# Forming P-Q on VectorE and GpSimd instead of in a third TensorE pass

## The chip, the cores and the metric

The kernel runs on one core of a Trainium2 chip. The metric is the device time of one execution in microseconds (us). The core's engines are TensorE (PE in the profile, with its weight loads as PEld), VectorE (DVE), ScalarE (ACT), GpSimd (POOL) and SyncE (SP). Each engine works through its own queue of instructions in the order of the program, and semaphores tie the queues together.

## The reference

```python
def _attn_ref(x):                       # x: (8, 3008, 256)
    X = np.fft.fft(x, axis=1)
    X = np.fft.fft(X, axis=2)
    return X.real

def _moe_ref(x, w_in, w_out):           # x: (24064, 256), w_in: (256, 2048), w_out: (2048, 256)
    h = np.maximum(x @ w_in, 0.0)
    return h * h @ w_out
```

The output of the first is reshaped to 24064 tokens of 256 and given to the second. So the real part of a two-dimensional Fourier transform of each of 8 batches goes through a feed-forward layer with a squared Relu.

## The kernel before

The real part of the transform splits into a part made of cosines, Zc, and a part made of sines, Zs. Row k of the result has P + Q as its product with `w_in`, and the mirrored row S - k has P - Q, where P comes from Zc and Q from Zs. The transform along the 256 dimensions is folded into the weights once: `gh[:, 0]` holds the cosine table times `w_in`, `gh[:, 1]` the sine table times `w_in`, each 128 x 2048, and `gh[:, 2]` is `gh[:, 1]` times -2. One row is different: partition 0 of Zs and of `gh[:, 1]` is used for the cosine part of d = 128, whose product has the same sign in both rows of a pair; there `gh[:, 2]` is 0 (`turn2`).

Columns. Only half of the 3008 rows of a batch are computed as columns (1505 a batch, 12040 in all); each column gives two rows of the output. The columns are cut into 25 windows: six of 240, 512, 376, 376, 512 and 448 columns (`FIRST`), then 18 full ones of 512 (windows 6 to 23, counted from 0) and a last one of 360.

A window. The hidden layer's 2048 features are 16 chunks of 128, handled in pairs by 8 pair steps, s = 0 to 7:

- `pq(s)`: for each of the two chunks a matmul of `gh[:, 0]` with Zc (`zcw`, L684) and one of `gh[:, 1]` with Zs (`zsw`, L685) into a PSUM tile `ph` of two banks: P + Q. There are two such tiles.
- `square(s, 0)`: ScalarE takes Relu of `ph` into `h1` (L694, three buffers), VectorE squares it into the first half of `h2` (L696).
- `others(s)`: work that is interleaved: steps of the fold of a later batch (`at[s]`), one eighth of the second matmul of the window before (`ffn2_steps`, L596; ScalarE copies two groups of its result at a time to `osb`, L611, and SyncE stores it), then `post[s]`, then matmuls that make Zc and Zs of the next window (`z_steps`, L478, L483, L487; VectorE's part is `minus`, L494).
- `turn(s)`: two matmuls of `gh[:, 2]` with Zs onto the same `ph` (L690), which makes it P - Q.
- `square(s, 1)`: Relu and square again, with the columns reversed, into the second half of `h2`.

The order is written out by hand (`manual_schedule`): each engine gets its instructions in the order of the program text.

The fold. Before its transform each batch is folded by symmetries into smaller inputs. In windows 5, 8, 10, 13, 16 and 19 (`fold_at`) a batch is folded beside the pair steps: step 0 has `d_even` (VectorE: `fe`, L349), step 1 `n_cos` (`ab`, L358), step 2 `d_odd` (`fo`, L353), step 3 `n_sin` (`ab`, L361), step 4 `odds` (`od`, L368). `d_odd` also issues the load of the next batch's `x` on GpSimd's queue (`load_x`, L125, L130, and L141 or L147 for batches at an edge), into a single buffer that `fo` is the last to read. `post[5]` has `nyq`: two small matmuls of TensorE on `od` (L373, L374). Step 6 has `even` (VectorE: `ev`, L379; GpSimd's queue stores it to DRAM as `scr`, L381), step 7 `back` (GpSimd's queue reads it back as `rb`, L389, L391). In windows 6, 9, 12, 15, 18 and 21 (`late_at`) steps 2 to 5 have the second stage of the fold (`fold8`, `fold16`, L404, L415, and small copies on GpSimd, L421 to L423).

Of the kernel before, what the change touches and what calls it, by code (L numbers as in the profile page):

```python
# [8 lines left out]
F32 = mybir.dt.float32  # L9
F16 = mybir.dt.float16  # L10
I32 = mybir.dt.int32
AF = mybir.ActivationFunctionType
ALU = mybir.AluOpType

HS = 32.0
P = 128
# [3 lines left out]
def rev_dim(ap, i):  # L20

    dims = [list(d) for d in ap.ap]
    step, cnt = dims[i]
    dims[i] = [-step, cnt]
    return bass.AP(tensor=ap.tensor, offset=ap.offset + step * (cnt - 1), ap=dims)
# [3 lines left out]
def kernel(  # L29
# [14 lines left out]
    nc = tc.nc  # L44
    B, S, D = x.shape
    _, F = moe_w_in.shape
# [7 lines left out]
    NFC = F // P  # L54
    WN = 512

    FIRST = [240, 512, 376, 376, 512, 448]
    R23 = float(2.0 ** 23)

    RQ = (1, 3, 5, 0, 2, 4)  # L60

# [11 lines left out]
    wins = []  # L73
# [5 lines left out]
    NW = len(wins)  # L79

    def win_of(col):
        return max(w for w in range(NW) if wins[w][0] <= col) if col < TOT else NW
# [17 lines left out]
    const = ctx.enter_context(tc.tile_pool(name="const", bufs=1))  # L100
    tmp = ctx.enter_context(tc.tile_pool(name="tmp", bufs=2))
# [7 lines left out]
    drp = ctx.enter_context(tc.tile_pool(name="drp", bufs=2, space=bass.MemoryType.DRAM))  # L109
    ps_h = ctx.enter_context(tc.tile_pool(name="ps_h", bufs=2, space=bass.MemoryType.PSUM))  # L110
    ps_o = ctx.enter_context(tc.tile_pool(name="ps_o", bufs=2, space=bass.MemoryType.PSUM))
# [56 lines left out]
    perm = [const.tile([P, P], F16, name=f"perm{i}") for i in range(2)]  # L168
# [3 lines left out]
    nc.gpsimd.memset(idx["c"][0:2, :], P - 3)  # L172
    idx["f"] = iota([P, 1], [[1, 1]], -1, 1, "idx_f")
    nc.gpsimd.memset(idx["f"][0:1, :], 0)
    w16 = [const.tile([P, 2, F // 2], F16, name=f"w16_{i}") for i in range(2)]
    for i in range(2):
        nc.gpsimd.dma_start(out=w16[i], in_=moe_w_in[:, i * F // 2 : (i + 1) * F // 2].rearrange("(c p) f -> p c f", p=P))
    wout16 = const.tile([P, NFC, D], F16, name="wout16")
# [2 lines left out]
    def small(shape, name):  # L181
        return const.tile(shape, F32, name=name)
# [22 lines left out]
    def table_steps(e):  # L205
# [19 lines left out]
        def args(h):  # L225
            t = st["t", h] = tmp.tile([P, 3, NE], F32, name="t", tag="tt")
            for j in range(nr):
                r = row(h, j)
                if e == 0:
                    nc.scalar.activation(t[:, j, 0:n], st["kf"], AF.Copy, bias=R23, scale=vs[:, r : r + 1])  # L230
                else:
                    nc.vector.tensor_scalar(out=t[:, j, 0:n], in0=st["kf"], scalar1=vs[:, r : r + 1], scalar2=R23, op0=ALU.mult, op1=ALU.add)

        def turns(h):
            t = st["t", h]
            nc.vector.tensor_scalar(out=t[:, 0:nr, 0:n], in0=t[:, 0:nr, 0:n], scalar1=-R23, scalar2=-float(S), op0=ALU.add, op1=ALU.mult)

# [44 lines left out]
    at = const.tile([P, 2, P + 1], F32, name="at")  # L282
    for c in range(2):
        nc.scalar.activation(at[:, c, :], drow, AF.Copy, bias=R23, scale=dvs[:, c : c + 1])
    nc.vector.tensor_scalar(out=at, in0=at, scalar1=-R23, scalar2=-float(D), op0=ALU.add, op1=ALU.mult)
    for c in range(2):
# [141 lines left out]
    gh = const.tile([P, 3, F], F16, name="gh")  # L428
# [17 lines left out]
    def gh_turn(cc):  # L446
        f0 = cc * 512
        nc.vector.tensor_scalar(out=gh[:, 2, f0 : f0 + 512], in0=gh[:, 1, f0 : f0 + 512], scalar1=turn2[:, 0:1], scalar2=None, op0=ALU.mult)
# [3 lines left out]
    def zwin(w):  # L452
        if w not in zc:
            zc[w] = zp.tile([P, WN], F16, name="zc", tag="zc")
            zs[w] = zp.tile([P, WN], F16, name="zs", tag="zs")
        return zc[w], zs[w]
# [101 lines left out]
    for cc in range(1, F // 512):  # L558
        gh_turn(cc)

    def store(osb, p0, g0, m, minus, eng=nc.sync):

        for b, k0, kstep, n, c0 in runs:
            il, ih = max(g0, c0) - c0, min(g0 + m, c0 + n) - 1 - c0
            if minus and k0 in (0, H):
                il = max(il, 1)
            cnt = ih - il + 1
            if cnt <= 0:
                continue
            if minus:  # L570
                lo = p0 + (m - 1) - (c0 + ih - g0)
                row = b * S + S - (k0 + kstep * ih)
            else:
                lo = p0 + c0 + il - g0
                row = b * S + k0 + kstep * il
            eng.dma_start(
                out=bass.AP(tensor=out.tensor, offset=out.offset + row * D, ap=[[kstep * D, cnt], [1, D]]),
                in_=osb[lo : lo + cnt, :])
# [51 lines left out]
    def fold_jobs(i):  # L630
        f = folds[i] = fold_steps(i)
        return [f["d_even"], f["n_cos"], f["d_odd"], f["n_sin"], f["odds"], f["nyq"], f["even"], f["back"]]

    fold_at, late_at = {}, {}
    for i in range(2, B):
        fold_at[win_of(col_of[i, 0]) - 2] = i
        late_at[win_of(col_of[i, 1]) - 2] = i
    NST = NFC // 2
    old = None
    for w in range(NW):  # L640
        g0, wn = wins[w]
        h2 = h2p.tile([P, NFC, 2 * WN], F16, name="h2", tag="h2")
        zcw, zsw = zwin(w)

        lo, hi = 0, NST - 1
        at = [[] for _ in range(NST)]
        post = [[] for _ in range(NST)]
        if w == 0:
            at[2] = [f0s["even"], f0s["back"]]
        elif w == 1:  # L650
            fj = fold_jobs(1)
            at = [[f] for f in fj[0:5]] + [[], [], []]
            post[5] = fj[5:6]
            lo, hi = 6, 7
        elif w == 2:
            te = table_steps(1)
            at = [[folds[1]["even"], lambda: te["freq"](), lambda: te["args"](0)], [lambda: te["turns"](0)], [lambda: te["mods"](0)],
                  [lambda: te["absm"](0)], [lambda: te["sins"](0)], [lambda: te["coss"](0)], [], [lambda: te["weigh"]()]]
            for st in range(4):
                at[st + 3] = at[st + 3] + f0s["late"][st : st + 1]  # L660
            at[7].append(folds[1]["back"])
        elif w in fold_at:
            fj = fold_jobs(fold_at[w])
            at = [[f] for f in fj[0:5]] + [[], fj[6:7], fj[7:8]]
            post[5] = fj[5:6]
        elif w == win_of(col_of[1, 1]) - 1:
            for st in range(4):
                at[st] = folds[1]["late"][st : st + 1]
            lo = 4
        if w in late_at:  # L670
            for st in range(4):
                at[st + 2] = at[st + 2] + folds[late_at[w]]["late"][st : st + 1]
        zj, zl = [], []
        for u in need[w + 1]:
            zu = z_steps(u)
            zj += [(zu, 0, 0), (zu, 1, 0), (zu, 0, 1), (zu, 1, 1)]
        f2 = ffn2_steps(*old) if old else []
        phs = {}

        def pq(s):  # L680
            ph = phs[s] = ps_h.tile([P, 2, 512], F32, name="ph", tag="psh")
            for a in range(2):
                f0 = (2 * s + a) * P
                nc.tensor.matmul(ph[:, a, 0:wn], gh[:, 0, f0 : f0 + P], zcw[:, 0:wn], start=True, stop=False)  # L684
                nc.tensor.matmul(ph[:, a, 0:wn], gh[:, 1, f0 : f0 + P], zsw[:, 0:wn], start=False, stop=True)  # L685

        def turn(s):
            for a in range(2):
                f0 = (2 * s + a) * P
                nc.tensor.matmul(phs[s][:, a, 0:wn], gh[:, 2, f0 : f0 + P], zsw[:, 0:wn], start=False, stop=True, skip_group_check=True)  # L690

        def square(s, sg):
            h1 = h1p.tile([P, 2, 512], F16, name="h1", tag="h1")
            nc.scalar.activation(h1[:, :, 0:wn], phs[s][:, :, 0:wn], AF.Relu)  # L694
            hv = rev_dim(h1[:, :, 0:wn], 2) if sg else h1[:, :, 0:wn]
            nc.vector.tensor_tensor(h2[:, 2 * s : 2 * s + 2, sg * wn : (sg + 1) * wn], hv, hv, op=ALU.mult)  # L696

        def others(s):
            for j in at[s]:
                j()  # L700
            for j in spread(f2, s, NST):
                j()
            for j in post[s]:
                j()
            if s == lo:
                zl[:] = [j for zu, part, h in zj for j in zu(part, h)]
            if s >= lo:
                for j in spread(zl, s - lo, hi - lo) if s < hi else []:
                    j()


        ng = 2 if w == 0 or wins[w - 1][1] < 384 < wn else 1
        for s0 in range(0, NST, ng):
            ss = range(s0, s0 + ng)
            for s in ss:
                pq(s)
            for s in ss:
                square(s, 0)
            others(s0)
            for s in ss:  # L720
                turn(s)
            for s in ss:
                square(s, 1)
            for s in ss[1:]:
                others(s)
        old = (w, h2)
    for j in ffn2_steps(*old, tail=True):
        j()
# [30 lines left out]
```

## Time and profile before

| | before |
|---|---|
| median of 3 runs | 633.65 us (633.65, 633.65, 635.58) |
| profiled execution, span from first to last instruction | 632.0 us |
| TensorE, matmuls | busy 615.9 us (97%) |
| ScalarE | busy 457.4 us (72%) |
| VectorE | busy 369.5 us (58%) |
| GpSimd | busy 76.5 us (12%), nearly all of it issuing DMAs |
| granted TensorE clock | 1.000 |

The time of the profiled execution itself is known as its span; the median of the runs is 1.65 us above it. A line of the profile's groups gives the source line, the engine, the operation, output and inputs by name, their shapes and the count, then the busy time, the mean duration of one instruction in ns, and the idle time of its engine before it with what ended that. A line of the timeline gives the start in us from the start of the span, the duration in us, the engine, the line, the operation and how many of them are merged, and in brackets the idle time before and its releaser. Matmuls are pipelined: one of 128x512 is shown with 379 ns, but the next starts 0.21 us after it.

### The profile page before, as it was taken

The page shows a single profiled execution, that of the slowest core. Times are in us where ns is not written, and L with a number is a line of the kernel's source. Part 1 is how long each engine was busy: PE and PEld are TensorE (multiplying, and loading weights), DVE is VectorE, ACT ScalarE, POOL GpSimd, SP SyncE. Part 2 cuts the span into 40 slices and gives each one's busy share as a digit, 9 for nine tenths or more (in the row PEclk, how much of TensorE's full clock was granted, in tenths as well). Part 3 has the DMA queues.
Part 4 walks back from the last instruction along what each step waited for, and adds up shares of the span by engine and source line. Part 5 has one row for each costly group of instructions (what it writes and reads, how often), then busy time and mean ns, then how long its engine had stood idle before and what let it go on. Part 6 is the DMA issues. An engine that isn't in the chain of part 4 may idle for free.

```text
span 632.0 us, 11586 instructions
## 1 busy us (share of the span) xinstructions
PE 615.9 (97%) x4548; PEld 439.1 (69%) x4548; DVE 369.5 (58%) x604; ACT 457.4 (72%) x610; POOL 76.5 (12%) x125
## 2 busy tenths in 40 slices
PE   5899999999999999999999999999999999999997
PEld 2457776776777767767777677777677776777786
DVE  7887656765457557645576455854557555454430
ACT  7787778777777677767777777777777777777662
POOL 5352200022002200220011100030000200000000
PEclk9999999999999999999999999999999999999999
DMA  8936211172112711631127211262111311111112
GB/s 146 211 82 127 85 34 34 50 164 78 36 43 58 184 46 42 144 97 35 51 44 160 74 52 39 59 151 73 40 31 55 111 34 47 38 46 35 49 54 65
DMA packets 36525, 47.52 MB, mean 75 GB/s; under 512 B 4216, under 2 KB 30328, under 8 KB 36472
## 3 DMA queue, kind: packets, MB, share of 16 engines
q0 software_dynamic: 9344, 22.14, 17.6%
q1 hardware_dynamic: 26899, 24.44, 12.7%
q8 instruction: 35, 0.57, 0.4%
q10 hardware_dynamic: 228, 0.21, 0.1%
q14 instruction: 19, 0.15, 0.1%
HBM read 33.63 MB, written 27.84 MB: 97 GB/s over the span
## 4 chain that ended last, share of the span: by engine, by line
PE 93%; DVE 3%; ACT 2%; issue 1%; POOL 0%; ACTq 0%; POOLq 0%; DVEq 0%
PE po L596 51%; PE ph L684 12%; PE ph L685 12%; PE ph L690 12%; PE pz L478 4%; ACT h L694 1%; PE pw L301 1%; DVE h L696 1%; PE pg L436 0%; ACT cos L259 0%; DVE fe L349 0%; DVE fo L353 0%; ACT sin L248 0%; ACT gh L440 0%; DVE od L368 0%
## 5 line engine op out<-in xcount | busy, mean ns | idle before, releaser
L694 ACT ACTIVATE h<-ph 128x1024 f16<-128x1024 f32 (+4 forms) x400 | 368.4, 974 | 80.0 <-PE ph L690 72.1
L696 DVE TENSOR_TENSOR h<-h 128x1024 f16<-128x1024 f16 (+4 forms) x400 | 262.4, 660 | 231.6 <-ACT h L694 228.2
L596 PE MATMUL po<-wout,h 128*128 128x256 f16 (+1 forms) x3024 | 361.6, 273 | 0.0
L596 PEld LDWEIGHTS <-h 128*128 128x128 f16 (+1 forms) x3024 | 296.8, 98 | 71.3
L684 PE MATMUL ph<-zc,gh 128*128 128x512 f16 (+4 forms) x400 | 145.9, 366 | 1.1 <-ACT h L694 0.8
L685 PE MATMUL ph<-zs,gh 128*128 128x512 f16 (+4 forms) x400 | 145.9, 366 | 0.4 <-ACT zs L487 0.4
L690 PE MATMUL ph<-zs,gh 128*128 128x512 f16 (+4 forms) x400 | 112.8, 366 | 2.0 <-ACT h L694 1.5
L611 ACT ACTIVATE osb<-po 128x512 f32<-128x512 f32 (+3 forms) x95 | 54.9, 582 | 57.4 <-PE po L596 52.4
L685 PEld LDWEIGHTS <-gh 128*128 128x128 f16 x400 | 39.1, 98 | 43.8 <-issue 2.5
L684 PEld LDWEIGHTS <-gh 128*128 128x128 f16 x400 | 39.0, 98 | 41.8 <-issue 0.5
L690 PEld LDWEIGHTS <-gh 128*128 128x128 f16 x400 | 37.2, 97 | 12.7 <-issue 4.3
L421 POOL COPY xt<-xt 128x2 f16<-128x2 f16 x16 | 2.5, 186 | 173.2 <-DVE xt L404 173.2
L130 POOL DMA_INDIRECT xo<-in_x_dram,idx_r x15 | 22.1, 1471 | 4.6 <-issue 4.6
L125 POOL DMA_DIRECT2D xo<-in_x_dram x8 | 6.0, 751 | 109.8 <-DVE fo L353 109.8
L483 ACT ACTIVATE es<-pz 128x376 f32<-128x376 f32 (+1 forms) x32 | 15.4, 481 | 5.3 <-PE pz L478 5.2
L391 POOL DMA_INDIRECT rb<-scr,idx_r x16 | 18.5, 1158 | 4.9 <-issue 4.9
L487 ACT ACTIVATE zs<-pz 128x376 f16<-128x376 f32 (+23 forms) x27 | 8.5, 358 | 9.9 <-PE pz L478 9.9
L349 DVE TENSOR_TENSOR fe<-xo 128x3072 f16<-128x3072 f16 x8 | 14.3, 1786 | 1.6 <-DMA xo<-in_x_dram,idx_r 1.3
L353 DVE TENSOR_TENSOR fo<-xo 128x3072 f16<-128x3072 f16 x8 | 14.2, 1779 | 0.0
L494 DVE SCALAR_TENSOR_TENSOR zc<-es,pz 128x376 f16<-128x376 f32 (+20 forms) x26 | 9.4, 392 | 7.2 <-ACT zc L487 7.0
L301 PE MATMUL pw<-spn 128*128 128x384 f16 x30 | 8.2, 448 | 5.2 <-DVE spn L290 5.2
L389 POOL DMA_DIRECT2D rb<-scr x16 | 8.8, 551 | 33.4 <-DMA scr<-ev 33.0
(106 smaller groups left out, 220.4 us busy)
## 6 DMA issues: line engine op xcount, KB each, us to landing
out_dram<-osb SPq DMA_DIRECT2D x77, 128.0 KB
xo<-in_x_dram POOLq DMA_DIRECT2D x7, 768.0 KB, 7.0
scr<-ev POOLq DMA_DIRECT2D x8, 390.0 KB, 4.4
rb<-scr POOLq DMA_DIRECT2D x16, 130.0 KB, 5.1
out_dram<-osb SPq DMA_DIRECT2D x12, 94.0 KB
w<-in_moe_w_in_dram POOLq DMA_DIRECT2D x2, 512.0 KB, 10.0
wout<-in_moe_w_out_dram POOLq DMA_DIRECT2D x1, 1024.0 KB, 14.5
out_dram<-osb SPq DMA_DIRECT2D x8, 75.0 KB
```

The lines of the kernel that those rows point to most:

```text
L130: nc.gpsimd.indirect_dma_start(out=flat(q), out_offset=None, in_=bass.AP(tensor=x.tensor, offset=0, ap=[[XW, B * S * D // XW], [1, XW]]), ...
L301: nc.tensor.matmul(pw[:, 0 : 3 * P], spn[:, 0, 0, :], spn.rearrange("p c r d -> p (c r d)")[:, 0 : 3 * P], start=True, stop=True)
L391: nc.gpsimd.indirect_dma_start(out=rb[:, q].rearrange("p r d -> p (r d)"), out_offset=None, in_=bass.AP(tensor=src.tensor, offset=src.offs ...
L478: nc.tensor.matmul(ps[:, o0:o1], lhs, tab, start=(h == 0 and k == 0), stop=last, skip_group_check=True)
L483: nc.scalar.activation(es[:, 0:n], ps[:, 0:n], AF.Copy, bias=0.0, scale=1.0)
L596: nc.tensor.matmul(po[0:m, j * D : (j + 1) * D], h2[:, fc, q : q + m], wout16[:, fc, :], start=(fc == 0), stop=(fc == NFC - 1))
L611: nc.scalar.activation(osb[0:mm].rearrange("p s d -> p (s d)")[:, lo:hi], po[0:mm, lo:hi], AF.Copy, bias=0.0, scale=HS * HS)
L684: nc.tensor.matmul(ph[:, a, 0:wn], gh[:, 0, f0 : f0 + P], zcw[:, 0:wn], start=True, stop=False)
L685: nc.tensor.matmul(ph[:, a, 0:wn], gh[:, 1, f0 : f0 + P], zsw[:, 0:wn], start=False, stop=True)
L690: nc.tensor.matmul(phs[s][:, a, 0:wn], gh[:, 2, f0 : f0 + P], zsw[:, 0:wn], start=False, stop=True, skip_group_check=True)
L694: nc.scalar.activation(h1[:, :, 0:wn], phs[s][:, :, 0:wn], AF.Relu)
L696: nc.vector.tensor_tensor(h2[:, 2 * s : 2 * s + 2, sg * wn : (sg + 1) * wn], hv, hv, op=ALU.mult)
```

## The change

In pair steps 1, 3 and 5 of the full windows 6 to 23, so 54 pair steps, `pq`, both `square`s and `turn` are replaced by two halves around `others(s)`.

`half_q`: the two Q matmuls alone go into `ph`; ScalarE copies -2Q from there to `sn[:, 0]` in SBUF; GpSimd makes the d = 128 products for the two chunks, twice row 0 of Zs (spread over the partitions, `eb`) times row 0 of `gh[:, 1]` (as a column, `wv`), in `sn[:, 1]`; VectorE adds them to `sn[:, 0]`.

`half_p`: the two P matmuls go onto the same `ph`, which makes P + Q; ScalarE copies it to the first half of `hd`; VectorE adds `sn[:, 0]` to it into the second half, reversed, which is P - Q; then VectorE takes the maximum with 0 of both halves and squares them into `h2`.

`wv` is made once, in step 0 of window 3 (`row_weights`: 16 matmuls of one column). `eb` is made once a window, at the end of the window before, by two DMAs on SyncE's queue: row 0 of Zs to DRAM, and from there to all partitions. `sn` uses the space of the two tiles `w16`, `hd` that of `tt` and `tm` (two buffers each), `eb` that of `kf` (two buffers).

```diff
+    MANY, FEW = (1, 3, 5), (1, 3, 5)
...
-    w16 = [const.tile([P, 2, F // 2], F16, name=f"w16_{i}") for i in range(2)]
+    w16 = [const.tile([P, 2, F // 2], F16, name=f"w16_{i}", tag=f"w16_{i}") for i in range(2)]
...
+    wv = small([P, NFC], "wv")
+
+    def row_weights():
+        pv = ps_o.tile([P, 512], F32, name="pv", tag="po")
+        for fc in range(NFC):
+            nc.tensor.matmul(pv[:, fc : fc + 1], gh[:, 1, fc * P : (fc + 1) * P], perm[0][:, P - 1 : P], start=True, stop=True)
+        nc.vector.tensor_copy(wv, pv[:, 0:NFC])
+
+    eb = {}
+
+    def row_spread(w):
+        wn = wins[w][1]
+        zr = drp.tile([1, WN], F16, name="zr", tag="zr")
+        nc.sync.dma_start(out=zr[0:1, 0:wn], in_=zwin(w)[1][0:1, 0:wn])
+        t = eb[w] = tmp.tile([P, WN], F16, name="eb", tag="kf")
+        src = zr[0:1, 0:wn]
+        nc.sync.dma_start(out=t[:, 0:wn], in_=bass.AP(tensor=src.tensor, offset=src.offset, ap=[[0, P], [1, wn]]))
...
+    def halved(w):
+        if wins[w][1] < WN or w < 6:
+            return ()
+        return FEW if w in fold_at else MANY
+
+    ROT = [0]
...
+        if w == 3:
+            at[0].append(row_weights)
...
+        two = halved(w)
+        sns, hds = {}, {}
+
+        def half_q(s):
+            ph = phs[s] = ps_h.tile([P, 2, 512], F32, name="ph", tag="psh")
+            for a in range(2):
+                f0 = (2 * s + a) * P
+                nc.tensor.matmul(ph[:, a, 0:wn], gh[:, 1, f0 : f0 + P], zsw[:, 0:wn], start=True, stop=True)
+            i = ROT[0] % 2
+            sn = sns[s] = const.tile([P, 2, 2, WN], F16, name=f"sn{i}", tag=f"w16_{i}")
+            nc.scalar.activation(sn[:, 0, :, 0:wn], ph[:, :, 0:wn], AF.Copy, bias=0.0, scale=-2.0)
+            for a in range(2):
+                nc.gpsimd.tensor_scalar(out=sn[:, 1, a, 0:wn], in0=eb[w][:, 0:wn], scalar1=wv[:, 2 * s + a : 2 * s + a + 1], scalar2=2.0, op0=ALU.mult, op1=ALU.mult)
+            nc.vector.tensor_tensor(sn[:, 0, :, 0:wn], sn[:, 0, :, 0:wn], sn[:, 1, :, 0:wn], op=ALU.add)
+
+        def half_p(s):
+            ph, sn = phs[s], sns[s]
+            for a in range(2):
+                f0 = (2 * s + a) * P
+                nc.tensor.matmul(ph[:, a, 0:wn], gh[:, 0, f0 : f0 + P], zcw[:, 0:wn], start=False, stop=True, skip_group_check=True)
+            hd = tmp.tile([P, 2, 2 * WN], F16, name="hd", tag=("tt", "tm")[ROT[0] % 2])
+            ROT[0] += 1
+            nc.scalar.activation(hd[:, :, 0:wn], ph[:, :, 0:wn], AF.Copy, bias=0.0, scale=1.0)
+            nc.vector.tensor_tensor(rev_dim(hd[:, :, wn : 2 * wn], 2), hd[:, :, 0:wn], sn[:, 0, :, 0:wn], op=ALU.add)
+            nc.vector.tensor_scalar(out=hd, in0=hd, scalar1=0.0, scalar2=None, op0=ALU.max)
+            nc.vector.tensor_tensor(h2[:, 2 * s : 2 * s + 2, :], hd, hd, op=ALU.mult)
...
         for s0 in range(0, NST, ng):
             ss = range(s0, s0 + ng)
+            if s0 in two:
+                half_q(s0)
+                others(s0)
+                half_p(s0)
+                continue
...
+        if w + 1 < NW and halved(w + 1):
+            row_spread(w + 1)
         old = (w, h2)
```

## The prediction

> **What bounds the kernel now.** I read the page's busy shares first, then the chain that ended last, then the timeline of a plain window, and last the stretch in which a batch is folded.
>
> ```profile
> PE 615.9 (97%) x4548; PEld 439.1 (69%) x4548; DVE 369.5 (58%) x604; ACT 457.4 (72%) x610; POOL 76.5 (12%) x125
> ...
> PE 93%; DVE 3%; ACT 2%; issue 1%; POOL 0%; ACTq 0%; POOLq 0%; DVEq 0%
> ```
>
> TensorE is busy for 97% of the 632.0 us span and is 93% of the chain: only a shorter TensorE stream can help, and any wait of TensorE adds its full length. One pair step of a full window, from the timeline:
>
> ```profile
> 301.63 0.59 PE L690 MATMUL ph<-zs,gh 128*128 128x512 f16 x2
> ...
> 302.06 0.38 PE L684 MATMUL ph<-zc,gh 128*128 128x512 f16 x1
> ...
> 302.26 1.94 ACT L694 ACTIVATE h<-ph 128x1024 f16<-128x1024 f32 x2 [1.04 <-PE ph L690]
> ...
> 302.93 1.91 PE L596 MATMUL po<-wout,h 128*128 128x256 f16 x16
> ...
> 304.68 0.59 PE L690 MATMUL ph<-zs,gh 128*128 128x512 f16 x2
> ...
> 305.11 0.38 PE L684 MATMUL ph<-zc,gh 128*128 128x512 f16 x1
> ```
>
> A step is 305.11 - 302.06 = 3.05 us of TensorE without a gap, of which the two turn matmuls (L690) take 302.06 - 301.63 = 0.43. ScalarE needs 1.94 plus half an output copy of 0.60, VectorE two squares of 0.69; they follow TensorE.
>
> The sixth batch is folded in window 13, whose first pair step starts at 317.27. GpSimd's part of the timeline there is whole:
>
> ```profile
> 328.81 0.75 POOL L125 DMA_DIRECT2D xo<-in_x_dram  x1 [16.99 <-DVE fo L353]
> 329.86 1.62 POOL L130 DMA_INDIRECT xo<-in_x_dram,idx_c  x1 [0.30 <-issue]
> 339.00 0.57 POOL L147 DMA_DIRECT2D xo<-in_x_dram  x1 [7.51 <-DMA xo<-in_x_dram,idx_c]
> 339.88 1.34 POOL L130 DMA_INDIRECT xo<-in_x_dram,idx_r  x1 [0.31 <-issue]
> 341.22 0.61 POOL L381 DMA_DIRECT2D scr<-ev  x1
> ```
>
> Of VectorE's and TensorE's parts, these:
>
> ```profile
> 326.73 1.78 DVE L353 TENSOR_TENSOR fo<-xo 128x3072 f16<-128x3072 f16 x1
> ...
> 333.15 0.97 DVE L368 TENSOR_TENSOR od<-ab 128x1548 f16<-128x1548 f16 x1
> ...
> 339.40 0.96 DVE L379 TENSOR_TENSOR ev<-ab 128x1560 f16<-128x1560 f16 x1
> ...
> 335.93 0.17 PE L373 MATMUL py<-od,perm 128*128 128x1 f16 x1
> ```
>
> GpSimd's queue is in order. The load of the next batch waits there for VectorE's fo, its buffer's last reader, then takes 12.4 us (328.81 to 341.22) with a wait for a gather in it. The store of ev stood behind it: its data were there at 340.36, and it went at 341.22, as the last gather ended. TensorE's nyq (L373) needs od, which VectorE had 1.8 us before (334.12 against 335.93).
>
> **The change, part by part.** Halved are pair steps 1, 3, 5 of the full windows 6 to 23: 18 x 3 = 54.
>
> TensorE: two turn matmuls go from each: 54 x 0.43 = -23.2 us. row_weights adds 16 weight loads with one-column matmuls, near 0.1 us each (LDWEIGHTS 98 ns): +1.6, once, with nothing to hide it.
>
> ScalarE: two copies of 128x1024 for two Relus of the same shape; the gh copy (L440) took 1024 ns against the Relu's 1026. Nothing. The P matmuls wait for the first copy: from the turn's end, 0.20 + 1.94 = 2.14 us, where TensorE comes after 0.43 + 1.73 = 2.16. Nothing to 0.1 us each; I take nothing.
>
> VectorE, per halved step: two adds at 0.69; the max over 2048, from L448 (512 elements, 349 ns) and L265 (377, 315), 0.25 ns an element: 0.74; the square over 2048, between ab (1560, 965 ns) and fe (3072, 1786): 1.23. That is 3.35 for 1.38: +1.97, x54 = 106 us on VectorE. In 25.4 us it is busy 14.5 now (271 us over 125 to 600); with 3 x 1.97 it has 20.4 of a window that TensorE ends in 24.1. So the average hides it; order does not, in the windows below.
>
> GpSimd: 108 products of 128x512. No row shows one. TENSOR_SCALAR takes 0.24 us at 2 elements. With the slope of IOTA (446 ns at 377, 260 at 128) 512 take 0.62; with the quicker perm row (518 ns at 128) 1.37; with the mean of the two perm rows (682) 2.05. I take 1.0, between IOTA, which reads nothing, and the quicker perm: 2.0 a step, ends 1.24 and 4.1.
>
> SP: two more transfers a window, one after the other, behind the window's last store: nothing else waits on SP but stores, which go after the second. The nearest hop is scr, 2.6 us from the end of its issue (213.46) to the wait's end (216.06); others took 4.4. So the copy of zs lands at about 0.3 + 2 x 2.6 = 5.5 in its window, and the first products end at X = 7.5. Bounds: 5.3, when ScalarE's own copy for step 1 is ready anyway, and 13.2 (hops of 4.4, slow products).
>
> Now the order. VectorE's add of step 1 stands ahead of all its later work, and so does that of step 3, whose products stand in GpSimd's queue behind the load of step 2. In a folding window VectorE does from X on: add 0.69, n_cos 0.96, add 0.69, max 0.74, square 1.23, Relu's square 0.69, fo 1.78 = 6.78. Only then does the load start, for L; then the products, 2.0; then add 0.69, n_sin 0.96, add 0.69, max 0.74, square 1.23, square 0.69, od 0.97 = 5.97. TensorE's nyq, in post of step 5, was due 335.93 - 317.27 = 18.7 into the window, and three turns earlier now: 17.4. Window 10, with L = 4.3 (252.68 to 257.00): 7.5 + 6.78 + 4.3 + 2.0 + 5.97 - 17.4 = 9.1 us of TensorE waiting. Window 8, L = 4.0: 8.8. Window 13, L = 12.4: 17.2. Window 16, L = 9.6 (404.92 to 414.48): 14.4. Window 19 loads nothing: 7.5 + 6.78 + 0.69 + 5.97 - 17.4 = 3.5. Together 53.0. Window 5 folds too, but has no halved step. Once od is there, TensorE has all it needs, and VectorE, with light steps 6 and 7 ahead, is not late again for the next window.
>
> In the other windows the late add at 7.5 is caught up by steps 6, 7 and 0, where VectorE has 1.38 in 3.05; I put them at nothing. If that cover went, each would cost the 2.2 by which the add is late. In a window after a fold the products also stand behind rb's transfers (over at 351.76, 8.9 into window 14, before): the add comes at 10.9, 5.6 late, against 24.1 - 20.4 = 3.7 of slack, so up to 1.9 each in four or five windows; I take nothing, since part of it falls where TensorE waits for nothing of VectorE's.
>
> Clock, from TensorE's timeline:
>
> ```profile
> 5.20 6.29 PE L301 MATMUL pw<-spn 128*128 128x384 f16 x20 [5.20 <-DVE spn L290]
> ...
> 14.19 0.81 PE L301 MATMUL pw<-spn 128*128 128x384 f16 x4
> ```
>
> The first 20 start 0.30 us apart ((6.29 - 0.53) / 19), four later ones 0.16, so a rested TensorE started at half rate and lost 20 x 0.14 = 2.8 us. TensorE waits for nothing longer than 1.0 us after that, so whether four waits of 9 to 17 us bring that back isn't shown: 0 to 2.8 each, the middle, 1.5, taken: +6. [...]
>
> Sum against the span: -23.2 + 1.6 + 53.0 + 6 = +37.4, so 632.0 becomes 669.4; the median of the runs lies 1.65 above the span: 671.
>
> **The rivals.** *Faster: the load does not hold the products.* If issuing leaves GpSimd free for arithmetic, the four L (30.3 us) fall out of 53.0 and the waits are too short for the clock. Then -23.2 + 1.6 + 22.7 = +1.1, and with quick products and X = 5.3 (14 less, below) -13: 621. The sign turns where the five waits sum to under 21.6. For it: GpSimd is 12% busy. Against it: the store of ev, held till the gather was out.
>
> *Slower still: VectorE and GpSimd get in each other's way.* If each holds the other off for a whole instruction, plain windows have 20.4 + 6 x 1.0 = 26.4 us of work for 24.1 of TensorE: 2.3 in each of 13 windows, +30, 701. The point is products of 0.62. The only such meeting in the trace, by the two lines' own answers (min/median/max in ns):
>
> ```profile
> L170 POOL TENSOR_SCALAR perm<-prow_i x2: 518/682/847, 5.4 to 6.2; 128x128 f16<-128x128 int32 x2
> L236 DVE TENSOR_SCALAR t<-t x3: 545/937/1057, 5.4 to 58.8; 128x1128 f32<-128x1128 f32 x2, 128x754 f32<-128x754 f32 x1
> ```
>
> Against the rival: L236 took 1057 ns beside both perm products and 937 without them, 0.12 more, not a whole product. For it: one of the products took 847 for 518. [...]
>
> *The removed pass was free.* Then -23.2 drops out: 694. The timeline excludes it: the turn's 0.43 stand in a stream without a gap, and the page has 2.0 us of idle time before all 400 matmuls of L690. Chance 0.
>
> **How the numbers follow.** Main case 0.70, 671. VectorE and GpSimd in each other's way 0.15, 701. Faster 0.13, 621. Within 0.3%, about what a measurement of this kernel can tell from no change, 0.02: that needs the waits to meet 21.6 by chance. The main case's low end has X = 5.3, products 1.24 and no clock loss: 5 x 2.2 + 4 x 0.76 = 14 less waiting, -20 with the clock: 651; and squares of 0.69 start 0.60 apart when nothing is between them, which takes about 1 us more from each of the five chains: 645. Its high end, X = 13.2 and products 4.1, gives 5 x 5.7 + 4 x 2.1 = 37 more: 708. The range 645 to 708 leaves out the faster case, no change, and some 0.05 above.
>
> **What the changed profile should show.** nyq (L373's successor) waiting for od by about 9, 9, 17, 14 and 3 us in five windows and TensorE idle there; GpSimd products of about 1 us, those of step 3 starting as the last gather of the load is issued; VectorE waiting for GpSimd in steps 1 and 3; plain windows of 24.1 us or a little over. Wrong is the forecast if products run while the load is pending, if od comes before 17.4 in a folding window, or if plain windows grow beyond 25.4.

## The result, and the profile after

| | before | after |
|---|---|---|
| median of the runs | 633.74 us | 706.98 us (704.09 to 710.14) |
| ratio of after to before, 95% interval | | 1.1152 (1.1117 to 1.1187) |
| profiled execution: time, span | span 632.0 us | 706.96 us, span 705.2 us |
| TensorE, matmuls | busy 615.9 us | busy 609.2 us |
| VectorE | busy 369.5 us | busy 481.7 us |
| GpSimd | busy 76.5 us | busy 188.8 us |
| granted TensorE clock, mean | 1.000 | 0.949 |

The change is slower by 11.5%. The forecast had the sign and 671 us; the time came 36 us higher, 1 us inside the upper end of the range (645 to 708). It lies nearer to the 701 of the rival "in each other's way" than to the forecast's own 671, so the time alone cannot tell the two apart; the windows and the runs below do. The page of after, in its order (busy time, clock in 40 slices, chain that ended last, groups):

```profile
PE 609.2 (86%) x4456; PEld 433.4 (61%) x4456; DVE 481.7 (68%) x713; ACT 459.4 (65%) x610; POOL 188.8 (27%) x233
...
PEclk9999999999997998999976999959999799999999
...
PE 42%; DVE 23%; DMA 15%; issue 10%; POOL 5%; ACT 3%; SPq 1%; DVEq 0%; ACTq 0%; POOLq 0%
...
L742 POOL TENSOR_SCALAR sn<-eb,wv 128x512 f16<-128x512 f16 x108 | 112.6, 1058 | 196.6 <-DMA eb<-zr 172.5
L743 DVE TENSOR_TENSOR sn<-sn 128x1024 f16<-128x1024 f16 x54 | 45.8, 848 | 111.7 <-POOL sn L742 111.7
...
L375 PE MATMUL py<-od,perm 128*128 128x1 f16 x8 | 1.3, 166 | 65.7 <-DVE od L370 65.7
```

TensorE was 93% of the chain and is 42% of it. What took the rest can be read in the last three lines: nyq (L375) waits 65.7 us for od; VectorE's add (L743) waits 111.7 us for GpSimd's products; and the products (L742) wait 172.5 us for the spread row `eb`. The slices of 5, 6 and 7 in the clock row are new.

Measured from the first P + Q matmul of one window to that of the next, the windows changed like this (us; plain windows were 24.3 to 26.2 long, folding ones 24.4 to 25.6):

| window | change | of it, nyq waiting for od | first add of the window starts at |
|---|---|---|---|
| 8 | +12.0 | 10.9 | 9.4 |
| 10 | +11.1 | 7.3 | 9.3 |
| 13 | +19.0 | 17.35 | 7.9 |
| 16 | +18.3 | 17.2 | 8.0 |
| 19 | +12.4 | 11.9 | 15.2 |
| 23 | +5.8 | | 14.6 |
| 7, 20, 11 | +1.0, +1.0, +0.5 | | 9.3, 13.1, 12.6 |
| the nine other plain windows | -0.6 to -1.3 each | | 7.1 to 11.0 |

So 72.7 of the 73.2 us by which the span grew lie in the five folding windows, and the gain of the plain ones is eaten by four of their own.

In window 8 (it starts at 191.6) GpSimd's timeline has the step that the forecast rested on, whole:

```profile
199.65 1.36 POOL L742 TENSOR_SCALAR sn<-eb,wv 128x512 f16<-128x512 f16 x2 [19.53 <-DMA eb<-zr]
207.81 0.80 POOL L127 DMA_DIRECT2D xo<-in_x_dram  x1 [6.79 <-DVE fo L355]
208.91 1.00 POOL L132 DMA_INDIRECT xo<-in_x_dram,idx_r  x1 [0.30 <-issue]
210.22 0.95 POOL L132 DMA_INDIRECT xo<-in_x_dram,idx_r  x1 [0.30 <-issue]
211.21 3.97 POOL L742 TENSOR_SCALAR sn<-eb,wv 128x512 f16<-128x512 f16 x4
```

VectorE and then TensorE in the same window:

```profile
212.61 1.22 DVE L743 TENSOR_TENSOR sn<-sn 128x1024 f16<-128x1024 f16 x1 [4.51 <-POOL sn L742]
...
218.23 0.97 DVE L370 TENSOR_TENSOR od<-ab 128x1548 f16<-128x1548 f16 x1
```

```profile
219.25 0.16 PE L375 MATMUL py<-od,perm 128*128 128x1 f16 x1 [10.90 <-DVE od L370]
```

Step 1's two products run at 199.65. Step 3's stand behind the load and start at 211.21, as its last gather has been issued. VectorE stands for 4.51 us before step 3's add, and od comes at 219.20. TensorE has waited 10.90 us for it.

### The profile page after: what moved, and what is told of

The parts are those of the page before. It is cut to its first block, busy times and chain, and to the rows that moved or that the text cites. A ratio compares the mean times of both kernels' runs of the same rounds, so it can differ in the third digit from the quotient of the medians.

```text
span 705.2 us, 11768 instructions
## 1 busy us (share of the span) xinstructions
PE 609.2 (86%) x4456; PEld 433.4 (61%) x4456; DVE 481.7 (68%) x713; ACT 459.4 (65%) x610; POOL 188.8 (27%) x233
## 4 chain that ended last, share of the span: by engine, by line
PE 42%; DVE 23%; DMA 15%; issue 10%; POOL 5%; ACT 3%; SPq 1%; DVEq 0%; ACTq 0%; POOLq 0%
PE po L618 24%; DVE h L728 6%; DMA zr<-zs 6%; DMA eb<-zr 5%; PE ph L716 5%; PE ph L717 5%; PE ph L722 4%; DVE hd L753 4%; DVE sn L743 4%; DVE hd L754 3%; POOL sn L742 2%; ACT h L726 2%; PE ph L749 2%; PE pz L480 2%; DVE fo L355 2%
## 5 line engine op out<-in xcount | busy, mean ns | idle before, releaser
L726 ACT ACTIVATE h<-ph 128x1024 f16<-128x1024 f32 (+4 forms) x292 | 270.9, 957 | 108.2 <-PE ph L722 65.9
L728 DVE TENSOR_TENSOR h<-h 128x1024 f16<-128x1024 f16 (+4 forms) x292 | 186.9, 655 | 80.3 <-ACT h L726 76.8
L742 POOL TENSOR_SCALAR sn<-eb,wv 128x512 f16<-128x512 f16 x108 | 112.6, 1058 | 196.6 <-DMA eb<-zr 172.5
L743 DVE TENSOR_TENSOR sn<-sn 128x1024 f16<-128x1024 f16 x54 | 45.8, 848 | 111.7 <-POOL sn L742 111.7
L717 PE MATMUL ph<-zs,gh 128*128 128x512 f16 (+4 forms) x292 | 108.0, 372 | 6.2 <-DVE zs L496 5.9
L716 PE MATMUL ph<-zc,gh 128*128 128x512 f16 (+4 forms) x292 | 108.0, 372 | 1.1 <-ACT h L726 0.8
L752 ACT ACTIVATE hd<-ph 128x1024 f16<-128x1024 f32 x54 | 55.5, 1028 | 63.9 <-PE ph L749 63.7
L722 PE MATMUL ph<-zs,gh 128*128 128x512 f16 (+4 forms) x292 | 80.7, 361 | 2.3 <-ACT h L726 1.5
L755 DVE TENSOR_TENSOR h<-hd 128x2048 f16<-128x2048 f16 x54 | 71.3, 1321 | 1.8
L375 PE MATMUL py<-od,perm 128*128 128x1 f16 x8 | 1.3, 166 | 65.7 <-DVE od L370 65.7
L740 ACT ACTIVATE sn<-ph 128x1024 f16<-128x1024 f32 x54 | 55.0, 1018 | 0.0
L753 DVE TENSOR_TENSOR hd<-hd,sn 128x1024 f16<-128x1024 f16 x54 | 43.1, 798 | 7.0 <-ACT hd L752 4.7
L749 PE MATMUL ph<-zc,gh 128*128 128x512 f16 x108 | 34.7, 405 | 7.7 <-ACT sn L740 7.7
L376 PEld LDWEIGHTS <-perm 128*128 128x128 f16 x8 | 0.8, 102 | 65.7 <-issue 65.5
L722 PEld LDWEIGHTS <-gh 128*128 128x128 f16 x292 | 27.2, 97 | 11.1 <-issue 5.0
## 6 DMA issues: line engine op xcount, KB each, us to landing
wout<-in_moe_w_out_dram POOLq DMA_DIRECT2D x1, 1024.0 KB, 14.3
```

The source lines that it names most:

```text
L742: nc.gpsimd.tensor_scalar(out=sn[:, 1, a, 0:wn], in0=eb[w][:, 0:wn], scalar1=wv[:, 2 * s + a : 2 * s + a + 1], scalar2=2.0, op0=ALU.mult, ...
L743: nc.vector.tensor_tensor(sn[:, 0, :, 0:wn], sn[:, 0, :, 0:wn], sn[:, 1, :, 0:wn], op=ALU.add)
L752: nc.scalar.activation(hd[:, :, 0:wn], ph[:, :, 0:wn], AF.Copy, bias=0.0, scale=1.0)
L753: nc.vector.tensor_tensor(rev_dim(hd[:, :, wn : 2 * wn], 2), hd[:, :, 0:wn], sn[:, 0, :, 0:wn], op=ALU.add)
L755: nc.vector.tensor_tensor(h2[:, 2 * s : 2 * s + 2, :], hd, hd, op=ALU.mult)
```

## The experiments

Theory: two things make od late, GpSimd's order (step 3's products behind the load) and the late row of Zs; the half clock after each wait adds to it. Rival: VectorE and GpSimd hold each other off, and that is the larger part. All medians stand beside a median of before of 633.9 to 635.05 us from the same chip; ratios are to before, with 95% intervals.

**prod_first: the products of steps 3 and 5 ahead of the load.**

```diff
+            if s == 1:
+                products(1)
+                products(3)
...
+                if s0 == 1:
+                    products(5)
```

> Same work, other order on GpSimd alone: the products of steps 3 and 5 are issued in step 1, ahead of the load of step 2. Theory (queue order): od no longer waits for the load; TensorE's wait for od falls from 7 to 17 us to 3 to 6 in windows 8, 10, 13 and 16 and stays near 12 in 19 (which loads nothing); with it goes the half clock in these four: 4 x 2.4. Together some 40 to 48 us less: 659 to 667. Rival (VectorE's longer chain and its meetings with GpSimd make the wait): the wait stays above 8 in each, 695 or more.

682.44 us, 1.0763 (1.0732 to 1.0794): 24.5 us less than after, but 15 above what the theory gave. Window 8 again, GpSimd:

```profile
199.14 3.93 POOL L739 TENSOR_SCALAR sn<-eb,wv 128x512 f16<-128x512 f16 x4 [19.49 <-DMA eb<-zr]
203.77 3.27 POOL L739 TENSOR_SCALAR sn<-eb,wv 128x512 f16<-128x512 f16 x2 [0.70 <-DVE hd L761]
208.97 0.80 POOL L127 DMA_DIRECT2D xo<-in_x_dram  x1 [1.93 <-DVE fo L355]
```

Now six products are done before the load starts. The waits for od fell from 64.7 us to 7.0, 3.3, 4.2, 4.9 and 11.8, together 31.1, which shows the order to be worth some 33 us of waiting. Window 19, which loads nothing, did not move (11.9 in after, 11.8 here): its wait has another cause. Two things kept the time above the theory's 667. Behind the shorter waits of windows 8, 10, 13 and 16 the granted clock still fell to 0.50, for 6.8, 3.4, 6.8 and 3.4 us, where the theory had it stay up. And window 11 was 7.8 us longer than before, for 0.5 in after: the second transfer of its row was issued 10.3 us after the first.

**eb_const: the row spread once.** All windows use window 6's row, so the d = 128 part is computed from the wrong row elsewhere.

```diff
-                nc.gpsimd.tensor_scalar(... in0=eb[w][:, 0:wn], ...)
+                nc.gpsimd.tensor_scalar(... in0=eb[6][:, 0:wn], ...)
...
-        if w + 1 < NW and halved(w + 1):
+        if w + 1 == 6:
```

> Row 0 of Zs is spread over the partitions once, for window 6, and that tile is used in all windows (the products are then those of window 6's row): no DMA round trip ahead of the products, which can be made in the window before. Theory (queue order): the load still holds the products of step 3, so TensorE still waits for od in windows 8, 10, 13 and 16, by 2 to 5 us less each; window 19's wait falls from 12 to about 3 and window 23 loses its 5.8: 675 to 685. Rival (the late row is the cause): the waits go, 615 to 635.

674.47 us, 1.0637 (1.0605 to 1.0669), half a microsecond below the expected band. Here window 19's wait fell from 11.9 to 1.9:

```profile
534.38 0.16 PE L375 MATMUL py<-od,perm 128*128 128x1 f16 x1 [1.94 <-DVE od L370]
```

Window 23 gained 1.3 instead of losing 5.8, and the other plain windows gained 1.1 to 1.3, but for window 7 (+3.2). In the windows with a load the waits stayed: 16.0 and 17.3 us in 13 and 16, 7.0 and 6.7 in 8 and 10. So the two causes are separate: the order makes the waits of the windows with a load, the late row makes window 19's and what the plain windows lose. All products run in this kernel and the plain windows still gain 1.1 to 1.3 us each: the rival would have had them grow.

**few_none: no halved step in the folding windows.**

```diff
-    MANY, FEW = (1, 3, 5), (1, 3, 5)
+    MANY, FEW = (1, 3, 5), ()
```

> The five folding windows 8, 10, 13, 16 and 19 go back to the full third pass; the other 13 full windows keep their halved steps. Theory (queue order: the products of step 3 stand behind the load of the next batch): in the trace of the changed kernel these five windows are 72.8 us longer than before and all others together 0.7 us shorter, so 707 - 73 = 634 us, within 3. Rival (VectorE and GpSimd are overloaded in every window, and folding windows only show it): the other windows stay where they are, but lateness that the folding windows passed on goes away or appears elsewhere: 634 plus or minus 10, with waits of TensorE in other windows.

658.11 us, 1.0379 (1.0349 to 1.0409): both theories missed, by 24 us from the 634 of each. The sign that the rival named, waits of TensorE in other windows, did come. Windows 8, 16 and 19 are as before to 0.4 us, 13 is +1.05 and 10 is +2.6. But windows 11, 17, 23, 20 and 7, all plain, lose 9.4, 6.8, 5.75, 3.1 and 2.7. In window 11 the row's second transfer is issued 15.0 us into the window, 9.5 after the first. So the row is not late by a fixed amount. That its lateness depends on where the stores lie, and that these moved, is an explanation that the sections below support; that it is the row and not overloaded engines follows from eb_const, where these plain windows, but for 7, gain.

**no_prod: no products.** The d = 128 part of a halved step is left out, and VectorE adds zeros of the same shape.

```diff
-            for a in range(2):
-                nc.gpsimd.tensor_scalar(...)
-            nc.vector.tensor_tensor(sn[:, 0, ...], sn[:, 0, ...], sn[:, 1, ...], op=ALU.add)
+            nc.vector.tensor_tensor(sn[:, 0, ...], sn[:, 0, ...], zero, op=ALU.add)
```

> The d = 128 products and the spreading of the row are left out; VectorE adds a tile of zeros in their place, so all its instructions stay and GpSimd has none of the new ones. Theory (queue order): nothing waits for GpSimd any more; what is left of the wait for od is VectorE's own longer chain, 1 to 3 us in five windows: 633.7 - 23.2 + 5 to 15 = 615 to 625. Rival (VectorE's longer chain): folding windows stay over 5 us longer than before, 640 or more.

618.68 us, 0.9757 (0.9729 to 0.9786), in the middle of what was expected. The plain windows end 1.27 to 1.30 us earlier, which is 3 x 0.43; the folding windows are level (+0.03 to +0.07, window 8 +0.36), their gain paid back by waits for od of 1.2 to 1.5 us. So TensorE's 0.43 a step is real; VectorE's added work alone costs 8.0 of the 23.2 us (633.9 - 618.7 = 15.2 are left), 7.0 of it in the five folding windows.

**idle_prod: no_prod, and GpSimd makes the 108 products from a constant tile, read by nobody.**

> As no_prod (VectorE adds zeros; 618.7 us, wait for od 1.2 us in folding windows), but GpSimd makes all 108 products from a constant tile and nobody reads them. Only the meeting of the two engines is left. Theory (products hold VectorE's two-operand instructions off for what is left of their 0.67 us, some 0.3 to 0.5 a product): VectorE's chain in folding windows about 0.5 to 1.5 later, plain windows nothing: 619 to 626. Rival (they do not meet): 618.7 within 1. Rival (they hold each other off so much that plain windows grow): 630 or more.

626.88 us, 0.9892 (0.9872 to 0.9912): 8.2 us more than no_prod, just above the theory's end and below the rival's. The groups of the two pages; the square is L755 in no_prod and L757 here:

```profile
L755 DVE TENSOR_TENSOR h<-hd 128x2048 f16<-128x2048 f16 x54 | 66.2, 1226 | 1.8
```

```profile
L742 POOL TENSOR_SCALAR sn<-eb,wv 128x512 f16<-128x512 f16 x108 | 139.6, 1306 | 81.4 <-DVE hd L755 81.1
L757 DVE TENSOR_TENSOR h<-hd 128x2048 f16<-128x2048 f16 x54 | 84.7, 1568 | 1.8
```

The mean square takes 1568 ns for 1226. So the engines do hold each other off, and here it costs 8.2 us, most of it in windows 18 (+2.7) and 10 (+2.2) by their length against before; most other windows keep their 1.3. An unread product still has to wait for its buffer (81.1 us in all, the end of the product's line above), so part of the 8.2 may be that.

**warm: after, with 550 unread matmuls of 128x256 ahead of nyq** in windows 8, 10, 13, 16 and 19 (90, 60, 150, 150, 100), so that TensorE is not at rest there.

> The changed kernel with 550 matmuls of 128x256 that nobody reads put ahead of nyq in windows 8, 10, 13, 16 and 19 (90, 60, 150, 150, 100 of them, 0.107 us each: less than the waits there). They fill the idle time and leave the waits as long. Theory (the half clock after a long wait of TensorE costs time by itself, 1.8 to 2.9 us in each of five windows): granted clock near 1 there, 707 - 12 = 695. Rival (the half clock falls in time that TensorE waits anyway): 705 to 709.

696.84 us, 1.0996 (1.0974 to 1.1018), 10.1 less than after and within 2 of what was expected; the mean clock is 0.993 for 0.949. The five windows grow by 10.0, 10.0, 16.3, 16.4 and 10.8, together 9.3 us less than in after. Work that is thrown away makes the kernel faster: the half clock behind the waits costs 9 to 10 us.

**few_none_early and pf_ebearly: the row spread at the start of step 7, ahead of the window's last stores,** in few_none and in prod_first.

```diff
+            if s == NST - 1 and w + 1 < NW and halved(w + 1):
+                row_spread(w + 1)
...
-        if w + 1 < NW and halved(w + 1):
-            row_spread(w + 1)
```

> As few_none (folding windows unhalved), and the spreading of row 0 of Zs is issued at the start of step 7, ahead of the last stores of its window, not behind them. In few_none the round trip of that row took 1.35 us from issue to issue where the stores ahead of it had 128 rows each, and 4 to 9.5 where one of them had a count such as 83, 113 or 117; windows with a late row were 2.6 to 9.4 us longer than before. Theory (the row stands behind such stores on SP's queue): all 13 halved windows become 1.0 to 1.3 us shorter than before: 633.9 - 16 = 618, within 3. Rival (VectorE and GpSimd holding each other off makes them late): windows with a late first add stay, 635 or more.

> All 54 halved steps, both orders mended: products of steps 3 and 5 ahead of the load, the row spread ahead of the last stores. Theory (queue order on GpSimd and on SP): plain windows 1.0 to 1.3 shorter than before, folding windows with a wait for od of 2 to 4 us, so 1 to 4 longer: 633.9 - 16 + 5 to 20 = 623 to 638. Rival (VectorE and GpSimd holding each other off): 650 or more.

few_none_early: 631.08 us, 0.9953 (0.9938 to 0.9969), 27 us below few_none and slightly faster than before, but 13 above the expected 618. pf_ebearly: 653.11 us, 1.0306 (1.0265 to 1.0347), 29 below prod_first, and on the rival's side of its bound. In both, windows 11 and 17 lose 3.3 to 5.2 us, and in pf_ebearly window 19 waits 9.4, each with the row still late (in few_none_early 7.4 and 9.1 us between its two issues). In pf_ebearly the windows 8, 10, 13 and 16 grow as well, by 2.1 to 4.6 us, with waits for od of 3.0 to 4.1, though the load holds nothing there any more.

**few_none_pool: few_none_early with both transfers on GpSimd's queue.**

```diff
-        nc.sync.dma_start(out=zr[0:1, 0:wn], ...)
+        nc.gpsimd.dma_start(out=zr[0:1, 0:wn], ...)
...
-        nc.sync.dma_start(out=t[:, 0:wn], ...)
+        nc.gpsimd.dma_start(out=t[:, 0:wn], ...)
```

> As few_none_early (only plain windows halved, the row spread from the start of step 7 of the window before), with both transfers of the row issued from GpSimd's queue instead of SyncE's. Theory (the first transfer waits behind output stores on SyncE's queue, and that alone makes the row late): none of the 13 halved windows is late, each ends 1.29 us earlier: 634 - 13 x 1.29 = 617, plus or minus 3. Rival (the transfers are slow wherever they are queued, because the DMA engines are busy with stores of few rows): windows 11 and 17 lose 4 to 5 us each as in few_none_early, 626 to 631.

626.7 us, 0.9884 (0.986 to 0.9908): a miss for the theory, and within the rival's time but not by its windows: 11 gains 1.3 and 17 is level. The answer on the tile `eb`:

```profile
L581 POOL DMA_DIRECT2D eb<-zr x13: 560/570/581, 144.2 to 565.6; - x13
...
  DMA zr<-zs: 45.2, 13
...
DMA to landing us min/median/max: 3.2/4.3/7.2
```

GpSimd waits 45.2 / 13 = 3.5 us on average for one row of 1 KB to land, and the second transfer takes 3.2 to 7.2. So SyncE's queue was a part of the delay, not the whole: window 17's two issues are still 7.4 us apart here, 9.1 there.

**bcast_few_none, bcast_pf, bcast_four: no transfer at all.** Row 0 of Zs is spread by one TensorE matmul with a matrix whose row 0 is ones and all else 0, and a ScalarE copy, in step 0 of the window itself. In bcast_few_none only plain windows are halved; bcast_pf has all 54 steps and prod_first's order; bcast_four halves step 6 of the plain windows too.

```diff
+        pb = ps_z.tile([P, 512], F32, name="pb", tag="pz")
+        nc.tensor.matmul(pb[:, 0:wn], sel, zwin(w)[1][:, 0:wn], start=True, stop=True)
         t = eb[w] = tmp.tile([P, WN], F16, name="eb", tag="kf")
+        nc.scalar.activation(t[:, 0:wn], pb[:, 0:wn], AF.Copy, bias=0.0, scale=1.0)
...
+            if s == 0 and two:
+                row_spread(w)
```

> Only the plain windows are halved (FEW empty), and the row of Zs is spread over the partitions by one TensorE matmul with a selector matrix and a ScalarE copy instead of two DMAs. Theory (the late row is what plain windows lose, and a few us of contention): no round trip, so each of the 18 windows with three halved steps ends 0.43 x 3 = 1.29 us earlier less 0.215 us for the added matmul: 633.9 - 18 x 1.07 = 614.6 at best; the windows that carry a fold are not halved and should be as before; 620, plus or minus 4. Rival (VectorE and GpSimd hold each other off, and that is the larger loss): 627 or more.

623.3 us, 0.9822 (0.9804 to 0.9839): within the band, and the fastest version that computes the reference. (The 614.6 of the expectation counts 18 halved windows where there are 13; 633.9 - 13 x 1.07 is 620, the middle of its band.) Its chain:

```profile
PE 89%; DVE 5%; DMA 1%; issue 1%; ACT 1%; POOL 1%; DVEq 0%; ACTq 0%; POOLq 0%
```

TensorE is the bound again. Twelve of the thirteen halved windows end 0.96 to 1.30 us earlier, the folding ones are as before, and only window 7 loses (+0.4, with a wait of 1.3 us for Zs).

> All 54 halved steps, products of steps 3 and 5 ahead of the load, and the row spread by the TensorE matmul. Theory: 633.9 - 54 x 0.43 + 0.215 x 18 = 614.6, plus five waits for od of 2 to 3 us in the folding windows: 622 to 630. Rival (holding off, or a wait that neither order nor row explains): 640 or more.

643.53 us, 1.0145 (1.0112 to 1.0179): 63.5 below after, but a miss by 14, on the rival's side. The windows say why, and it isn't what the rival means. The plain ones, but for 7, 14, 17 and 18, gain 1.05 to 1.29. The folding ones grow by 2.7, 3.5, 1.8, 3.5 and 1.8: in each the first add starts at 6.3 and od is there at 20.4, while TensorE wanted it 2.7 to 3.6 us earlier, and in two of them, 10 and 16, TensorE then has 3.4 us at half clock. That is the forecast's chain with the load and step 3's products taken out, 6.3 + 6.78 + 5.97 = 19.1; the 1.3 us that are left may be meetings of the two engines, which no run separates here. Windows 14 and 17 lose 3.0 and 1.6 with waits of 2.3 and 2.5; their products start 12.0 and 12.2 us into the window, behind rb's transfers.

> As bcast_few_none, with four halved steps (1, 3, 5, 6) in a plain window instead of three. Theory (VectorE has room in plain windows): 0.43 us less for each added halved step, 5 to 6 us below bcast_few_none, so 614 to 616. Rival (VectorE's added 1.97 us for each becomes the bound, or GpSimd's products do): no lower than bcast_few_none.

637.9 us, 1.0062 (1.0045 to 1.008): slower than with three steps by 14.6 and than before by 0.6%. The profiled execution was the fastest of the six, 633.67, so its trace shows the smaller part of the loss. Its chain, and the line that took the place:

```profile
PE 74%; DVE 16%; issue 4%; ACT 3%; POOL 2%; DVEq 0%; POOLq 0%; ACTq 0%
```

```profile
L621 PE MATMUL po<-wout,h 128*128 128x256 f16 (+1 forms) x3024 | 367.3, 274 | 9.2 <-DVE h L758 7.5
```

TensorE's second matmul waits for the square of a halved step (L758). In windows 11, 14, 17 and 20 the fourth step brings its 0.43 (-1.5 against -1.08), but windows 7, 10, 13, 16, 18 and 19 grow by 1.1 to 3.3 and 12 and 15 gain nothing: VectorE's squares of the window before reach into them. So a fourth halved step does not fit behind VectorE as it stands. Whether it would without the meetings of the two engines is not shown: the square took 1417 ns on average here and 1348 with three steps, for 1226 in no_prod.

## Why the prediction was right or wrong

It forecast +37.4 on the span and the trace has +73.2. The step that carried it held; two sizes and one zero did not. That the time still fell inside the range is luck: the upper end of 708 adds 37 us for rows as late as 13.2 and products of 4.1 us a step in all five folding windows, while of the 35.8 us that were missing only 11.7 lie in waits for od, and two products took 1.4 us where nothing met them.

**The load holds the products: right, nearly to the number.** Window 13, forecast against trace: first add at 7.5, 7.9; fo done at 14.3, 14.4; step 3's products from 26.7, 26.9; od done at 34.7, 34.9; wait 17.2, 17.35. That it meets to 0.2 is partly luck: step 3's add began 1.4 us after its products did, for the 2.0 taken, and the chain from that add to od took 6.55, for 5.97. The rival "faster, the load does not hold the products" is excluded by the timeline above and by prod_first. In window 16 the load held 12.0 us instead of the 9.6 taken from before, which is 2.4 of its 2.8 of excess.

**The removed pass: right.** no_prod's plain windows end 1.27 to 1.30 earlier, 3 x 0.43.

**The copies of the row: mis-sized, and the largest error.** "Two hops of 2.6" put the first products' end at 7.5 with a bound of 13.2. The trace has the add between 7.1 and 15.2, outside the bound in windows 19 and 23. The bound was too low by the forecast's own source: the same timeline of GpSimd has hops of scr of 5.8 and 6.3 us, in windows 10 and 13, beside the 2.6 and 4.4. The cause is the sentence "behind the window's last store: nothing else waits on SP but stores": it asked who waits for the row's transfers, not what their data queue behind. SyncE's queue in window 23 and in window 18 of after:

```profile
640.71 2.69 SPq L578 DMA_DIRECT2D zr<-zs  x1
648.90 0.35 SPq L581 DMA_DIRECT2D eb<-zr  x1
```

```profile
503.78 0.25 SPq L578 DMA_DIRECT2D zr<-zs  x1
505.22 0.33 SPq L581 DMA_DIRECT2D eb<-zr  x1
```

The second transfer waits for the first: 8.2 us in the one, 1.4 in the other. What the DMA engines moved, in 40 slices from 636 to 650 and from 499 to 506:

```profile
GB/s 47 47 50 50 32 47 26 12 0 0 0 114 114 50 18 12 12 18 23 23 23 23 26 23 23 26 23 23 23 73 23 23 23 26 23 6 0 0 0 29
```

```profile
GB/s 29 18 18 23 23 23 23 23 23 23 29 23 23 23 23 23 23 23 29 23 23 23 23 23 23 23 59 322 316 158 345 310 29 0 0 0 0 0 0 0
```

The last stores ahead of the row had 75, 53, 15 and 113 rows of 1 KB in window 23 and 128 and 128 in window 18. The first kind moves at about 23 GB/s for the 8 us that the row waits; the second at over 300, and the row comes through at once (the 23 GB/s ahead of them are, by their order, stores of 61 and 67 rows). From 643.5 to 648.5 the 16 DMA engines are busy for 0.08 of the time on average, which is 1.3 engines. The number of rows alone does not sort the 18 windows: behind 84, 44 and 128 rows (window 16) the two issues were 1.5 us apart, behind 53, 75 and 128 (window 19) 5.4. What decides which stores leave at 23 GB/s is not shown.

Over the 18 windows of after the two issues were 1.1 to 8.2 us apart. No run changed the rows of a store, so that the row waits behind the stores that leave slowly is argued, from their place ahead of it and from the rate while it waits, and not shown. Its place in SyncE's queue is not all of it: on GpSimd's queue (few_none_pool) the first hop still took 3.5 us on average.

**"In the other windows nothing": wrong.** The plain windows should have given 13 x 1.29 = 16.8 us and gave 0.8: window 23 lost 5.8, 7 and 20 one each. The forecast's own test, plain windows beyond 25.4, is met by windows 7, 11, 20 and 23 (26.5, 26.7, 27.3 and 30.1, for 25.5, 26.2, 26.2 and 24.3 before, so that three of the four lay beyond it already). The mechanism it had priced at 2.2 for a late add was there, but with an add at 13 to 15 it takes TensorE, not VectorE's slack. Without the transfers (bcast_few_none) the zero is nearly right.

**Window 19: 3.5 forecast, 11.9 measured,** from an add at 15.2 for 7.5. With the row constant it was 1.9.

**The clock: +6 forecast, 9 to 10 measured** (warm). The middle between 0 and 2.8 a wait was too low: it took 1.9 to 2.0 us on average for each of the five. In window 8 of after TensorE waited from 208.35 to 219.25, and the granted clock was 0.50 from about 213.6, inside the wait, to 223.8, some 4.6 us after it. The length of a wait alone does not decide it: in bcast_pf the trace has 3.4 us at half clock behind waits of 2.74, 2.25 and 2.69 us in windows 10, 14 and 16, and none behind 3.56, 2.74 and 2.69 in windows 8, 13 and 19. That the five waits of the rival "faster", 3.5 to 4.8 us each by its sum, are too short for the clock was the author's estimate; in prod_first 3.3 to 4.9 us in windows 10, 13 and 16 brought 3.4, 6.8 and 3.4 us at 0.50.

**Smaller terms.** A product takes 0.70 us in the median, 0.68 at least (1.0 taken; the mean with its meetings is 1.06); the max takes 0.69 (0.74), the square 1.23 (1.23), row_weights' window grows by 0.17 (1.6 forecast).

The sum, 35.8 us off: plain windows 16.0, waits for od 64.7 for 53.0, or 11.7, half clock 3.3 (9.3), a wait for Zs in window 10 of 2.6, row_weights -1.4, 1.1 ahead of the first window and behind the last, and 2.6 in the folding windows that no view here assigns.

**The rival "in each other's way": the mechanism exists, its price was not this one.** VectorE in window 18 of after, first beside the products and then without any:

```profile
509.92 1.17 DVE L743 TENSOR_TENSOR sn<-sn 128x1024 f16<-128x1024 f16 x1 [2.47 <-POOL sn L742]
...
512.95 1.60 DVE L755 TENSOR_TENSOR h<-hd 128x2048 f16<-128x2048 f16 x1
...
516.69 0.68 DVE L743 TENSOR_TENSOR sn<-sn 128x1024 f16<-128x1024 f16 x1
...
519.35 1.23 DVE L755 TENSOR_TENSOR h<-hd 128x2048 f16<-128x2048 f16 x1
```

```profile
508.52 3.13 POOL L742 TENSOR_SCALAR sn<-eb,wv 128x512 f16<-128x512 f16 x4 [16.53 <-DMA eb<-zr]
512.35 3.27 POOL L742 TENSOR_SCALAR sn<-eb,wv 128x512 f16<-128x512 f16 x2 [0.70 <-DVE hd L753]
```

The same add takes 1.17 us beside a product and 0.68 alone, the square 1.60 and 1.23, and two products, 0.68 us each when alone, stretch to 3.27. But the rival had it cost 2.3 us in each of 13 plain windows, and in eb_const and bcast_few_none, with all products running, nearly all of these gain their 1.1 to 1.3. Its price is some 8 us where it was measured (idle_prod), not 30. Part of the 8 may be waits of the products for their buffer. The sum above leaves no 30 us for it either.

## What to carry to other kernels

Of an instruction or a transfer that is added to an in-order queue, ask both questions: who waits behind it, and what it waits behind; the forecast asked the first of GpSimd and got its waits to 0.2 us in one window, partly by luck, and failed to ask the second of SyncE. A value that a nearer engine can spread (here one 0.215 us matmul and a copy) was worth more here than a free-looking round trip through DRAM whose first hop varied by 7 us in after. And take a change apart by window before judging it: with the row spread by TensorE, halved steps in the 13 plain windows alone made the kernel 1.8% faster; with the five folding windows halved too, where VectorE's longer chain makes od late, it was 1.5% slower.

## What the runs showed of the hardware that was not expected

- Behind two stores of 128 rows of 1 KB the DMA engines moved over 300 GB/s, and the DMA that waits for a 1 KB transfer queued behind them was issued 1.4 us after it; behind stores of 75, 53, 15 and 113 rows they moved about 23 GB/s for most of the time, and it was issued 8.2 us after.
- One row of 1 KB through DRAM and out to 128 partitions, on GpSimd's queue, took 3.5 us for the first hop on average (wait only) and 3.2 to 7.2 us for the second.
- 550 matmuls whose result is thrown away made the kernel 10.1 us faster; the mean granted clock was 0.993 with them and 0.949 without.
- Half clock followed waits of TensorE as short as 2.25 us in bcast_pf, and did not follow one of 3.56 us in the same trace.
